# State update of a chunked delta-rule attention: one product chain for both halves of the heads, two copies of the state

## The chip, the core and the metric

The kernel runs on one core of a Trainium2 chip. The metric is the device time in microseconds (us), the median of three runs. The engines are PE (TensorE matmul; PEld is its weight load), DVE (VectorE), ACT (ScalarE), POOL (GpSimd) and SP (SyncE, whose queue issues the DMAs).

## The reference

Three stages follow one another. The first is a recurrent attention over 768 tokens for 4 batches of 8 heads, head size 48, with a state of 48 x 48 per head:

```python
k_n = k / (np.linalg.norm(k, axis=-1, keepdims=True) + 1e-06)
for t in range(S):
    kt, vt, bt = (k_n[:, :, t], v[:, :, t], beta[:, :, t, None])
    y[:, :, t] = np.einsum('bhd,bhde->bhe', q[:, :, t], state)
    v_old = np.einsum('bhde,bhd->bhe', state, kt)
    state = state + bt[:, :, :, None] * np.einsum('bhd,bhe->bhde', kt, vt - v_old)
```

Its output, as 3072 rows of 384, goes through a soft mixture of 8 experts (32 slots; the softmax over the tokens needs all of them first) and then through a feed-forward layer of width 2048 with a leaky ReLU. All arrays are float32.

## The kernel before

**Steps.** The 768 tokens are cut into 24 steps of 32. The partitions of most tiles are 4 batches times 32 tokens. The 8 heads are two halves of four, A = 0 and A = 1, and the batches two pairs, bp = 0 and bp = 1. Inside a step the recurrence over its 32 tokens is replaced by a triangular inverse, which does not depend on the state, so that one step is a chain of products. For each half:

- `ks_mm` (L406): ks(A), the step's keys times the state S[A], 16 matmuls, which the trace records as 32, added in PSUM (tile `ksu[A]`) to the values that `seed` (L399, ACT) put there.
- `z_of` (L423, L424 on ACT, L426 on DVE): the result is split into a high and a low fp16 part.
- `u_mm` (L432): the inverse, loaded into `tmb`, times z, 12 matmuls; then `u` is split in two fp16 parts too, u[:, 0] by L437 on ACT, and, up to step 19, u[:, 1] by a correcting matmul (L439) and a second ACT copy (L440). From step 20 on DVE makes u[:, 1] (L442).
- `s_mm` (L452): the state product. Keys (`khb`, high and low) times u (high and low) in three passes, `PASSB`: key high by u[:, 0], key low by u[:, 0], key high by u[:, 1]. Each pass has 4 heads times 2 batch pairs, so 8 matmuls on 64 rows each, alternately on rows 0 to 63 and 64 to 127 of the array (the two row tiles). They accumulate over all steps into two PSUM banks, `sps[0]` and `sps[1]`, one for each batch pair; both halves lie in each bank, in columns of their own.
- Two ACT copies (L456), 128x192 each, one for each bank, bring the half's new S to SBUF for the next step's `ks_mm` and `qs_mm`.
- `qs_mm` (L417, L413 from step 16) and `mu_mm` (L463, 24 matmuls for both halves) make the output `y`; `mu_mm` stands behind the last state product by `issue_after(last_s[0])`. L826 on ACT copies y; `logits` transposes it (L470), copies it (L473, ACT) and multiplies it by phi (L480), one step late. `soft` (among others L501, L510, L513, L517) does the running softmax of each four steps.

Beside the chain lies `gram` (L200, PE), eight steps ahead up to step 15, which yields the matrices to invert, and their copies (L207, L216).

**The inverse.** Four steps make a group. `solve(g)` inverts the matrices of a group on DVE (L241 to L312, with few ACT instructions, L250, L251, L316); it is a generator, and each `yield` ends a piece. solve(1) has 64 pieces: 8 up to the row of norms (L282), then one or two for each column j of the elimination (from column 3 on the first piece is L301 and L287, the second L305), at the end a transposition (L308) and the fp16 parts (L316 on ACT, L312 on DVE). `bs.run(n)` puts the next n pieces into the program. `DQ` tells how many at each of eight places of a step: place 0 is ahead of step 0, places 1 to 7 lie behind z(0), behind the DMAs, behind u(0), ahead of and between the two state products, behind the step's loads and at its end. At step 2 of a group `bs.run()` takes all that is left. So before the change solve(1) has 8 pieces ahead of step 0, 16 in step 0, 16 in step 1, and 24 in step 2; its result is first used in step 4. Solves of groups 2 to 5 begin in steps 3, 7, 11 and 15. From step 19 on DVE also decodes 64-bit weights (L560, L561, L563, L593 to L603).

**What sets the order.** The text of the program is not the order of an engine. A planner with a cost model of its own lists the instructions of each engine, by due time and priority: `tc.high_priority(offset=...)` moves a block ahead (dictionary `P`: `st`, the state product and its copies, 300; `mu` 300; `x` -30; `dma` -300), `tc.issue_after(i)` forbids an instruction to stand ahead of i on i's engine, and `behind(...)` does so for instructions noted in `end`. On the chip each engine keeps that order and waits where an operand isn't there.

**DMA.** All loads are issued by SP in one list: for each step two of keys and queries (`kqb`), four of the inverse (`tmb`, L380), four of the keys (`khb`, L369), one of keys and values (L329), and for later steps one to three more (L180, L189). `load_kq` is held until the last state product, `load_kv` until the last `u_mm` of half 0. From step 16 on the weights of the later stages are loaded (L571 and others; L632 brings the experts' w1 and w2, from step 20 on).

**After the attention** come the experts (L913, L932), fed by weights from memory, and the feed-forward layer (L1015, L1053 to L1068), which is a dense row of matmuls.

The loop over s in 0 to 23 contains, in this order: ks(0), preparation for step s + 2, `bs.run(dq[1])`, gram, ks(1), `step_dma`, `bs.run(dq[2])`, `qs_mm` of both halves, u(0), `bs.run(dq[3])`, u(1), both seeds, `soft`, `bs.run(dq[4])`, `s_mm` of half 0, `bs.run(dq[5])`, `s_mm` of half 1, loads, `bs.run(dq[6])`, the logits, `mu_mm`, L826, `bs.run(dq[7])`.

Of the kernel before, what the change touches and what calls it, by code (L numbers as in the profile page):

```python
# [8 lines left out]
F32 = mybir.dt.float32  # L9
# [3 lines left out]
AF = mybir.ActivationFunctionType  # L13
# [4 lines left out]
NST = 24  # L18
# [2 lines left out]
P = dict(st=300, mu=300, x=-30, dma=-300, split=-30, wi=-100)  # L21
DQ = (8, 5, 2, 2, 2, 2, 2, 1)
DQ_LAST = (8, 2, 3, 3, 3, 3, 3, 3)
DQ_NEXT = (0, 0, 1, 1, 1, 1, 1, 0)
DQ_FIRST = (0, 5, 2, 2, 3, 3, 3, 2)
SOFT_POOL = 5
# [18 lines left out]
PASSB = ((0, 0), (1, 0), (0, 1))  # L45


def drain(gen):
    for _ in gen:
        pass  # L50
# [3 lines left out]
def fused_kernel(ctx: ExitStack, tc: tile.TileContext, kq, kv, bu, phi, w1, w2, wi, wo, out):  # L54
    nc = tc.nc
    ve, sc, gp, pe, sy = nc.vector, nc.scalar, nc.gpsimd, nc.tensor, nc.sync

    def pool(stack, name, bufs, **kw):
        return stack.enter_context(tc.tile_pool(name=name, bufs=bufs, **kw))
# [14 lines left out]
    p_s = pool(at, "s", 2)  # L74
# [83 lines left out]
    def behind(*keys):  # L158
        st = ExitStack()
        for k in keys:  # L160
            if k in end:
                st.enter_context(tc.issue_after(end[k]))
        return st
# [170 lines left out]
    khs, last_s, tms = {}, [None], {}  # L334
# [20 lines left out]
    def step_k(s):  # L355
        khc = p_w.tile([128, 2, 384], F16, tag="khc", name="khc", bufs=KB)
        k1 = kvs[s // 2][:, s % 2, 0]
        sc.activation(k1, k1, AF.Copy, scale=64.0)
        kv1 = k1.rearrange("p (d a h) -> p a d h", a=2, h=4)
        k0, kl = [khc[:, l].rearrange("p (a d h) -> p a d h", a=2, h=4) for l in range(2)]  # L360
        end["k"] = sc.activation(k0, kv1, AF.Copy).ins
        after_solve(gp.tensor_tensor(kl, kv1, k0, SUB), s)
        khs[s] = khc.rearrange("p l (a x) -> p (l a) x", a=2)
# [19 lines left out]
    spf = [ps_st.tile([128, 512], F32, name=f"sps{i}") for i in range(2)]  # L383
    sps = [t[:, 0:384].rearrange("p (a h e) -> p a h e", a=2, h=4) for t in spf]
# [8 lines left out]
    S = {}  # L393
# [7 lines left out]
    def ks_mm(s, A):  # L401
        kb, st = kqb[s % 2], S[A]
        for hh in range(4):
            for b in range(4):
                bp, r = b // 2, slice(32 * (b % 2), 32 * (b % 2) + 32)
                end["ks"] = pe.matmul(ksu[A][32 * b:32 * b + 32, 48 * hh:48 * hh + 48], kb[:, bp, 0, r, 4 * A + hh], st[:, bp, hh, :],  # L406
                          start=False, stop=True, skip_group_check=True).ins
# [12 lines left out]
    def z_of(s, A):  # L420
        z = p_w.tile([128, 3, 192], F16, tag=f"z{A}", name="z")
        zp = ksu[A][:, 0:192]
        sc.activation(z[:, 0], zp, AF.Copy, scale=2.0 ** -6)  # L423
        end["z"] = sc.activation(z[:, 2], zp, AF.Copy, scale=2.0 ** -17).ins  # L424
        with behind("p") if s and s % 4 == 0 and s < 20 else nullcontext():
            end["zd"] = ve.scalar_tensor_tensor(z[:, 1], zp, 2.0 ** -6, z[:, 0], MULT, SUB).ins  # L426
        return z
# [14 lines left out]
            ve.scalar_tensor_tensor(u[:, 1], up, 32.0, u[:, 0], MULT, SUB)  # L442
        return u

    def s_mm(s, A, u):
        kb = khb[:, s % 2]
        for i, (a, b) in enumerate(PASSB):
            for hh in range(4):
                for bp in range(2):
                    q = slice(64 * bp, 64 * bp + 64)  # L450
                    with tc.issue_after(last_u[A].ins), tc.issue_after(last_s[0]) if last_s[0] is not None else nullcontext():
                        last_s[0] = pe.matmul(sps[bp][:, A, hh, :], kb[q, a, A, :, hh], u[q, b, hh, :],  # L452
                              start=False, stop=(s == NST - 2 and i == 2), skip_group_check=True).ins
        st = p_s.tile([128, 2, 4, 48], F32, tag=f"s{A}", name="st")
        for bp in range(2):
            sc.activation(st[:, bp], sps[bp][:, A], AF.Copy)  # L456
        S[A] = st

    def mu_mm(s, A, u, y):
        mv = tmb[s % 2][:, 2:4]  # L460
# [136 lines left out]
    def conv_wi(q):  # L597
        t = W[0, q] = place(3 * q, [128, 2, 768], F16)
        top = top_of(q < len(RAW), q)
        yield from from_f64(raw64.pop(("i", q)), top)  # L600
        sc.activation(t[:, 0], top, AF.Copy, scale=1024.0)
        yield
        ve.scalar_tensor_tensor(t[:, 1], top, 1024.0, t[:, 0], MULT, SUB)  # L603
        yield
# [36 lines left out]
    def load_late(s):  # L641
        with tc.issue_after(last_dma[0]):
            for x in LOADS.get(s, ()):
                if x == "w":
                    load_w()
                elif x == "i":
                    load_wi(n_wi[0])
                    n_wi[0] += 1
                else:
                    load_wo(n_wo[0])  # L650
                    n_wo[0] += 1

    def prep(s):
        step_m(s)
        step_ew(s)

    def pri(n):
        return tc.high_priority(offset=P[n]) if n in P else nullcontext()
# [78 lines left out]
    for s in range(NST):  # L737
        y = ps_y.tile([128, 8, 48], F32, tag="y", name="y")
        z, u = {}, {}
        dq = DQ_NEXT if s % 4 == 3 else DQ_FIRST if s and s % 4 == 0 else DQ if s < 15 else DQ_LAST  # L740

        def ks(A):
            if s:
                ks_mm(s, A)
            z[A] = z_of(s, A) if s else first_z[A]

        with behind("mu", "lp", "x"):
            ks(0)
        with behind("z"):
            if s + 2 < NST:  # L750
                prep(s + 2)
            if s + 2 < NST - 1:
                step_k(s + 2)
        with behind("zd"):
            bs.run(dq[1])
        if s + GA < NST:
            with behind("ks"):
                drain(gram(s + GA, masks))
        with behind("gm", "k"):
            ks(1)  # L760
        with behind("zd"):
            while masks:
                masks.pop()()
        if s in (3, 7, 11, 15):
            bs.add(solve(s // 4 + 2))
        if s == 19:
            load_late(s)
        if s + 1 < NST:
            with pri("dma"):
                step_dma(s + 1)  # L770
        if s != 19:
            load_late(s)
        for x, q in CONV.get(s, ()):
            bc.add(conv_wi(q) if x == "i" else conv_wo(q))

        def conv(n=1):
            if bc.q:
                with pri("wi"), tc.issue_after(solved[NG - 1]):
                    bc.run(n)
        with behind("zd"):  # L780
            bs.run(dq[2])
        if s:
            with behind("ks"):
                qs_mm(s, 0, y)
                qs_mm(s, 1, y)
        lg = logits(s - 1) if s else iter(())
        with behind("y"):
            u[0] = u_mm(s, 0, z[0])
            bs.run(dq[3])
            u[1] = u_mm(s, 1, z[1])  # L790
            with behind("u"):
                next(lg, None)
            if s < NST - 1:
                for A in range(2):
                    seed(s + 1, A)
            if s > 4:
                bf.run((0, 1, 2, 9)[s % 4])
            conv()
            bs.run(dq[4])
            if s < NST - 1:  # L800
                with pri("st"):
                    s_mm(s, 0, u[0])
            conv()
            bs.run(dq[5])
            if s < NST - 1:
                with pri("st"):
                    s_mm(s, 1, u[1])
        with tc.issue_after(tms[s + (s % 4 == 3 and s + 1 < NST)]):
            if s + 4 < NST:
                load_kv(s + 4, last_u[0].ins)  # L810
        with tc.issue_after(tms[s]):
            if s + 1 < NST - 1:
                with pri("dma"):
                    step_kdma(s + 1)
            if s + 10 < NST:
                load_kq(s + 10, last_s[0])
        conv()
        bs.run(dq[6])
        with behind("y"), tc.issue_after(last_s[0]):
            drain(lg)  # L820
            with pri("mu"), tc.issue_after(last_s[0]):
                for A in range(2):
                    mu_mm(s, A, u[A], y)
        with pri("x"):
            x = xg[s // 4 % 2][:, s % 4]
            end["x"] = sc.activation(x, y.rearrange("p h e -> p (h e)"), AF.Copy, scale=2.0 ** -12).ins  # L826
        if s % 4 == 2:
            bs.run()
        conv()
        bs.run(dq[7])  # L830
        if s and s % 4 == 0:
            bf.add(soft(s // 4 - 1))
            bf.run(1)
        free.extend(AVAIL.get(s, ()))
# [132 lines left out]
    with tc.high_priority(offset=CHAIN_PRIO), tc.issue_after(conv_ins[0]):  # L967
# [10 lines left out]
        for c in range(3):  # L978
            x = ss[:, c].unsqueeze(1).to_broadcast([128, 4, 32])
            h, l = [so16[:, i, c].rearrange("p (r x) -> p r x", r=4) for i in range(2)]  # L980
# [134 lines left out]
```

## Time and profile before

| what | us |
|---|---|
| median of three runs | 605.42 (601.75 to 609.35) |
| the profiled execution: its own time | 606.53 |
| its span, first to last instruction | 604.8 |
| outside the span | 1.7 |

PE is busy for 513.0 us of the span (85%), DVE 364.1 (60%), ACT 322.2 (53%), POOL 206.0 (34%). "PEclk" in a row is the granted TensorE clock as a share of 2.4 GHz: 1.00 is that level, 0.50 is 1.2 GHz, and what lies between is a stretch with both. Steps are told apart here by where ks(0) of a step begins; step 5, for example, goes from 105.61 to 117.32 us.

How such rows are read: a timeline row has the start, the time from the first to the last of the instructions that it merges, engine, line, what is written from what, and in brackets the idle time of the engine ahead of it and what ended it. A row of waits has the total of such idle times, how many there were and the longest. In rows by windows the busy times of the five engines stand behind the window's length.

### The profile page before, as it was taken

Reading aid. Unit: us, or ns where it says so; the run is one execution under the profiler, and the core shown is the slowest. Engines: PE = TensorE matmul, PEld = TensorE weight load, DVE = VectorE, ACT = ScalarE, POOL = GpSimd, SP = SyncE. Lnnn points to the kernel's source line nnn. Section 1 sums busy time; section 2 is a strip of 40 time slices with the busy share of each in tenths; the row PEclk is TensorE's granted clock in tenths of the full one; section 3 lists DMA queues with packets and bytes.
Section 4 is the critical chain, followed back from the end, with each engine's and each line's share of the span. In section 5 each row is a group of like instructions: output and inputs, shape, how many; then the busy total and the mean of one; then the engine's idle time right before and its main releaser. Section 6 shows DMA issues by size and latency. Waiting matters only on the chain.

```text
span 604.8 us, 18636 instructions
## 1 busy us (share of the span) xinstructions
PE 513.0 (85%) x7650; PEld 365.9 (60%) x7650; DVE 364.1 (60%) x1020; ACT 322.2 (53%) x783; POOL 206.0 (34%) x206
## 2 busy tenths in 40 slices
PE   7516787998987987888676978899999999999996
PEld 5515686877877875776674422566555555555553
DVE  3799778789887777899614453886423242333331
ACT  1325466566666655666542152566656555555552
POOL 9404122222313222224201000255555555454542
PEclk9665689899898787786687799999999999999999
DMA  9956658658766536786689999310101010010101
GB/s 221 227 124 152 144 137 194 155 140 191 171 172 161 131 90 156 201 260 128 193 267 420 395 404 418 143 53 1 53 0 54 2 42 12 1 54 1 53 1 52
DMA packets 70964, 87.27 MB, mean 144 GB/s; under 512 B 42720, under 2 KB 59360, under 8 KB 70880
## 3 DMA queue, kind: packets, MB, share of 16 engines
q1 hardware_dynamic: 70880, 86.09, 49.7%
q8 instruction: 60, 0.98, 0.7%
q14 instruction: 24, 0.20, 0.1%
HBM read 70.53 MB, written 4.72 MB: 124 GB/s over the span
## 4 chain that ended last, share of the span: by engine, by line
PE 63%; DVE 19%; ACT 8%; DMA 6%; issue 3%; SPq 0%; DVEq 0%; POOL 0%; ACTq 0%; POOLq 0%
PE ops L1015 31%; PE gm L200 4%; DMA arena<-in_w_dram 4%; PE hps L1053 3%; PE sps L452 3%; PE y L463 3%; PE xq L480 3%; PE ksu L406 3%; PE ksu L432 2%; DVE arena L301 2%; DVE arena L305 2%; DVE arena L287 2%; DMA kv<-in_kv_dram 2%; DVE arena L274 1%; ACT ksu L399 1%
## 5 line engine op out<-in xcount | busy, mean ns | idle before, releaser
L1068 POOL TENSOR_TENSOR gl<-gf,gh 128x512 f16<-128x512 f32 x96 | 113.7, 1200 | 151.4 <-ACT gh L1067 77.7
L1015 PE MATMUL ops<-late,gh 128*128 128x384 f16 x768 | 144.1, 326 | 0.0
L1062 DVE SCALAR_TENSOR_TENSOR gf<-hps,hs 128x512 f32<-128x512 f32 x96 | 62.5, 686 | 110.9 <-ACT hs L1061 110.7
L1015 PEld LDWEIGHTS <-gh 128*128 128x128 f16 x768 | 75.1, 98 | 53.6 <-ACT gh L1067 0.3
L1061 ACT ACTIVATE hs<-hps 128x512 f32<-128x512 f32 x96 | 53.0, 594 | 56.1 <-PE hps L1053 55.8
L1015 PE MATMUL ops<-late,gl 128*128 128x384 f16 x384 | 81.7, 326 | 0.0
L1067 ACT ACTIVATE gh<-gf 128x512 f16<-128x512 f32 x96 | 60.4, 629 | 26.7 <-DVE gf L1062 20.4
L352 POOL TENSOR_TENSOR vsz<-kv,nn 128x384 f32<-128x384 f32 x24 | 23.7, 988 | 101.9 <-issue 60.1
L200 PE MATMUL gm<-kqr,arena 128*64 128x64 f32 x640 | 44.2, 311 | 16.0 <-issue 16.0
L301 DVE TENSOR_TENSOR arena<-arena 128x81 f32<-128x81 f32 (+12 forms) x150 | 57.4, 383 | 0.1
L452 PE MATMUL sps<-u,khb 64*128 64x48 f16 x1104 | 35.1, 197 | 25.5 <-ACT st L456 20.6
L305 DVE TENSOR_TENSOR arena<-arena 128x81 f32<-128x81 f32 (+12 forms) x150 | 53.2, 355 | 0.0
L1015 PEld LDWEIGHTS <-gl 128*128 128x128 f16 x384 | 37.6, 98 | 24.8
L200 PEld LDWEIGHTS gm<-kqr,arena 128*64 128x64 f32 x640 | 41.2, 221 | 18.1 <-issue 16.2
L452 PEld LDWEIGHTS <-khb 64*128 64x128 f16 x1104 | 26.8, 115 | 38.2 <-issue 32.2
L406 PE MATMUL ksu<-st,kqb 128*32 128x48 f32 x1472 | 47.8, 258 | 2.5 <-issue 1.3
L346 POOL TENSOR_TENSOR tc<-mm,tc 128x256 f16<-128x256 f32 x24 | 19.4, 807 | 82.7 <-ACT tc L345 59.4
L287 DVE SCALAR_TENSOR_TENSOR arena<-arena 128x28 f32<-128x28 f32 (+27 forms) x186 | 47.0, 263 | 0.4
L406 PEld LDWEIGHTS ksu<-st,kqb 128*32 128x32 f32 x1472 | 39.6, 156 | 5.1 <-issue 1.4
L426 DVE SCALAR_TENSOR_TENSOR z<-ksu,z 128x192 f16<-128x192 f32 x48 | 16.8, 351 | 35.1 <-ACT z L424 35.0
L432 PE MATMUL ksu<-z,tmb 128*128 128x48 f16 x576 | 26.8, 195 | 9.2 <-DVE z L426 8.9
L432 PEld LDWEIGHTS <-tmb 128*128 128x128 f16 x576 | 23.8, 118 | 13.6 <-issue 10.8
(176 smaller groups left out, 856.9 us busy)
## 6 DMA issues: line engine op xcount, KB each, us to landing
we<-in_w_dram SPq DMA_DIRECT2D x22, 768.0 KB, 10.4
kv<-in_kv_dram SPq DMA_DIRECT2D x24, 384.0 KB, 4.5
kqb<-in_kq_dram SPq DMA_DIRECT2D x46, 192.0 KB, 4.3
kqr<-in_kq_dram SPq DMA_DIRECT2D x20, 384.0 KB, 4.8
arena<-in_w_dram SPq DMA_DIRECT2D x10, 768.0 KB, 8.3
tmb<-tc SPq DMA_DIRECT2D x96, 64.0 KB, 3.0
arena<-in_wi_dram SPq DMA_DIRECT2D x6, 768.0 KB, 6.4
raw<-in_wo_dram SPq DMA_DIRECT2D x6, 768.0 KB, 9.6
```

The source lines that it names most:

```text
L200: end["gm"] = pe.matmul(gm[64 * bp:64 * bp + 64, h, :], kb[:, k, bp, :, h], c[:, k, bp, :, :, h], start=(h == 0), stop=True, skip_group_ch ...
L287: end["p"] = ve.scalar_tensor_tensor(R[:, i, 0:j], R[:, j, 0:j], gu[:, i, j:j + 1], R[:, i, 0:j], MULT, ADD).ins
L301: ve.tensor_tensor(tv, gu[:, j + 2:, j:j + 1].to_broadcast([128, n, w]), R[:, j:j + 1, 0:w].to_broadcast([128, n, w]), MULT)
L305: ve.tensor_tensor(R[:, j + 2:, 0:w], R[:, j + 2:, 0:w], tv, ADD)
L406: end["ks"] = pe.matmul(ksu[A][32 * b:32 * b + 32, 48 * hh:48 * hh + 48], kb[:, bp, 0, r, 4 * A + hh], st[:, bp, hh, :], start=False, stop ...
L432: last_u[A] = pe.matmul(ksu[A][:, 192 + 48 * hh:240 + 48 * hh], tmb[s % 2][:, a, A, :, hh], z[:, b, 48 * hh:48 * hh + 48], start=False, st ...
L452: last_s[0] = pe.matmul(sps[bp][:, A, hh, :], kb[q, a, A, :, hh], u[q, b, hh, :], start=False, stop=(s == NST - 2 and i == 2), skip_group_ ...
L1015: pe.matmul(ops[t], g[:, 128 * t:128 * t + 128], w, start=(ft == 0 and i == 0), stop=(ft == 15 and i == 2))
L1061: sc.activation(hs, hps, AF.Copy, scale=2.0 ** -12)
L1062: gf_ins = ve.scalar_tensor_tensor(gf, hps, 0.01 * 2.0 ** -12, hs, MULT, MAX).ins
L1067: sc.activation(gh, gf, AF.Copy)
L1068: gp.tensor_tensor(gl, gf, gh, SUB)
```

## The change

Three things change. `s_mm` is called once in a step, behind the place where half 1's product stood, and writes the products of both halves in one chain, in the order half 0 passes 0 and 1, half 1 passes 0 and 1, half 0 pass 2, half 1 pass 2; the number of matmuls stays 48. S of both halves is one tile, copied by two ACT instructions of 128x384, one for each bank, instead of four of 128x192. And solve(1) gets other numbers of pieces: 10 in step 0 (4, 1, 1, 1, 1, 1, 1 at places 1 to 7) and 21 in step 1 (2, 4, 3, 3, 3, 3, 3), with 25 left for step 2; all other steps keep theirs.

```diff
+DQ_BEGIN = ((0, 4, 1, 1, 1, 1, 1, 1), (0, 2, 4, 3, 3, 3, 3, 3))
...
-    def s_mm(s, A, u):
+    def s_mm(s, u):
         kb = khb[:, s % 2]
-        for i, (a, b) in enumerate(PASSB):
+        for A, i in ((0, 0), (0, 1), (1, 0), (1, 1), (0, 2), (1, 2)):
+            a, b = PASSB[i]
             for hh in range(4):
                 for bp in range(2):
                     q = slice(64 * bp, 64 * bp + 64)
                     with tc.issue_after(last_u[A].ins), tc.issue_after(last_s[0]) if last_s[0] is not None else nullcontext():
-                        last_s[0] = pe.matmul(sps[bp][:, A, hh, :], kb[q, a, A, :, hh], u[q, b, hh, :],
+                        last_s[0] = pe.matmul(sps[bp][:, A, hh, :], kb[q, a, A, :, hh], u[A][q, b, hh, :],
                               start=False, stop=(s == NST - 2 and i == 2), skip_group_check=True).ins
-        st = p_s.tile([128, 2, 4, 48], F32, tag=f"s{A}", name="st")
+        st = p_s.tile([128, 2, 2, 4, 48], F32, tag="s", name="st")
         for bp in range(2):
-            sc.activation(st[:, bp], sps[bp][:, A], AF.Copy)
-        S[A] = st
+            sc.activation(st[:, bp].rearrange("p a h e -> p (a h e)"), spf[bp][:, 0:384], AF.Copy)
+        for A in range(2):
+            S[A] = st[:, :, A]
...
-        dq = DQ_NEXT if s % 4 == 3 else DQ_FIRST if s and s % 4 == 0 else DQ if s < 15 else DQ_LAST
+        dq = DQ_BEGIN[s] if s < 2 else DQ_NEXT if s % 4 == 3 else DQ_FIRST if s and s % 4 == 0 else DQ if s < 15 else DQ_LAST
...
             bs.run(dq[4])
-            if s < NST - 1:
-                with pri("st"):
-                    s_mm(s, 0, u[0])
             conv()
             bs.run(dq[5])
             if s < NST - 1:
                 with pri("st"):
-                    s_mm(s, 1, u[1])
+                    s_mm(s, u)
```

## Rows read from the trace of the kernel before

**Rows 1.** Waits of PE, 45 to 330 us: total us, times, longest us.
```profile
PE sps L452 <- ACT st L456: 20.6, 19, 1.3
...
PE ksu L432 <- DVE z L426: 8.9, 10, 3.1
PE mq L517 <- DVE acc L513: 4.5, 3, 1.6
```

**Rows 2.** Windows by stage: busy PE, PEld, DVE, ACT, POOL; PEclk, DMA share, GB/s.
```profile
48.84:320.79 271.95, 225.93 (x5688) 198.19 (x5688) 208.18 (x685) 162.71 (x491) 67.26 (x79) 0.82 0.68 174
320.79:381.00 60.21, 48.02 (x377) 20.67 (x375) 29.56 (x73) 21.70 (x45) 2.54 (x3) 0.90 0.99 399
```

**Rows 3.** Timeline of step 5: start, length, engine, line, what, count, [idle, releaser].
```profile
113.10 0.31 PE L452 MATMUL sps<-u,khb 64*128 64x48 f16 x8
...
113.43 0.48 ACT L473 ACTIVATE xt<-xq 128x384 f32<-128x384 f32 x1
...
113.80 0.50 ACT L399 ACTIVATE ksu<-vsz 128x384 f32<-128x384 f32 x1
...
114.21 0.56 ACT L456 ACTIVATE st<-sps 128x192 f32<-128x192 f32 x2
...
114.60 0.85 PE L452 MATMUL sps<-u,khb 64*128 64x48 f16 x24 [1.19 <-ACT st L456]
...
115.38 1.15 PE L463 MATMUL y<-u,tmb 128*128 128x48 f16 x24
...
117.32 0.39 PE L406 MATMUL ksu<-st,kqb 128*32 128x48 f32 x6
```

**Rows 4.** Waits of L452: steps 8 and 9; 16 to 18; 20 to 22.
```profile
  ACT st L456: 2.3, 2
...
  ACT st L456: 3.5, 3
...
  ACT st L456: 2.2, 3
```

**Rows 5.** Windows: steps 8 and 9; 16 to 18; 19 and 20.
```profile
138.17:161.55 23.38, 19.96 (x539) 17.86 (x537) 21.97 (x84) 15.04 (x48) 7.25 (x9) 0.88 0.85 200
...
233.93:266.32 32.39, 26.99 (x612) 23.90 (x610) 28.15 (x108) 18.79 (x60) 8.61 (x10) 0.76 0.75 198
266.32:296.29 29.97, 21.90 (x415) 17.13 (x415) 26.70 (x39) 18.50 (x49) 10.73 (x8) 0.67 0.71 196
```

**Rows 6.** Timeline of step 1, and where step 2 begins on DVE.
```profile
60.91 0.33 ACT L424 ACTIVATE z<-ksu 128x192 f16<-128x192 f32 x1
...
61.85 0.33 DVE L301 TENSOR_TENSOR arena<-arena 128x176 f32<-128x176 f32 x1
...
65.00 0.34 DVE L426 SCALAR_TENSOR_TENSOR z<-ksu,z 128x192 f16<-128x192 f32 x1
...
65.39 0.64 PE L432 MATMUL ksu<-z,tmb 128*128 128x48 f16 x12 [3.10 <-DVE z L426]
...
73.78 0.36 DVE L426 SCALAR_TENSOR_TENSOR z<-ksu,z 128x192 f16<-128x192 f32 x1 [3.94 <-ACT z L424]
```

**Rows 7.** Timeline of step 18: product, copies of S, next ks(0).
```profile
264.14 0.78 PE L452 MATMUL sps<-u,khb 64*128 64x48 f16 x24 [1.18 <-ACT st L456]
...
266.32 0.38 PE L406 MATMUL ksu<-st,kqb 128*32 128x48 f32 x2
...
267.79 1.15 ACT L316 ACTIVATE tc<-arena 128x256 f16<-128x256 f32 x2 [3.09 <-DVE arena L308]
...
268.84 0.53 ACT L456 ACTIVATE st<-sps 128x192 f32<-128x192 f32 x2
```

**Rows 8.** Windows from state product's end to next ks(0)'s end, steps 5, 6.
```profile
115.45:118.53 3.08, 3.08 (x64) 2.77 (x64) 1.40 (x4) 1.05 (x3) 0.71 (x1) 0.53 0.83 229
126.90:129.06 2.16, 2.16 (x64) 2.07 (x64) 2.06 (x9) 1.04 (x3) 0.79 (x1) 1.00 0.25 77
```

**Rows 9.** View of waits, the DMA queue of SP, steps 0 to 22.
```profile
SPq L369 <- PE sps L452: 34.1, 14, 6.0
```

## The prediction

> **What bounds the kernel now.** I read the windows by stage first, then the waits of PE, then the timeline of one step. The steps of the attention last 271.95 us, in which PE is busy 225.93 [rows 2]: PE is the busiest engine, and 46 us of its time there is idle. DVE follows with 208.18. Behind the steps 60.21 us run with the DMA engines 0.99 busy: that stretch starts when the steps end and is not touched. The waits say who makes PE idle: the largest by far is the state product behind its own copies, 20.6 us in 19 waits; then come u_mm behind the z of DVE, 8.9 us, and a transposition of the softmax behind DVE's L513, 4.5 us [rows 1].
>
> Step 5 shows the first wait [rows 3]. Half 0's product is written by 113.41 us (113.10 and 0.31 us). Half 1's product, into other columns of the same two banks, starts at 114.60 only, 1.19 us idle, released by the copy of half 0. That copy does not start until 114.21, because ACT works off the copy of L473 (113.43) and a seed (113.80) first. So on each step PE stands still for ACT, with half 1's operands at hand.
>
> **The wait removed.** In one chain no copy stands between the halves; with the same 48 matmuls it ends the wait earlier, at 114.60 + 0.85 - 1.19 = 114.26 [rows 3]. Of the 20.6 us, by place:
> - Steps 20 to 22: 2.2 us [rows 4]. Steps 19 and 20 together are held by DVE, 26.70 of 29.97 us busy with decoding [rows 5], and behind them the full DMA stretch follows. I count 0 (bounds 0 and 2.2).
> - Steps 16 to 18: 3.5 us [rows 4]. DVE is busy 28.15 of 32.39 us there [rows 5], with 4.2 us left over, not all of it where it is needed. I count half, 1.7 (0 to 3.5).
> - Steps 8 and 9: 2.3 us [rows 4], but DVE has only 23.38 - 21.97 = 1.4 us left [rows 5]. I count 1.4 (0 to 2.3).
> - The other 11 waits: 20.6 - 2.2 - 3.5 - 2.3 = 12.6 us. I count 12.3 (12.6 at most, and 6 if DVE took half of them too); step 0 has no logits that would cover the later copy, and keeps some 0.3 of its wait.
>
> Together 15.4 us.
>
> **The copies, later and wider.** Half 0's S now comes behind the whole chain, and ks(0) of the next step needs it. The cover is what PE does first: mu_mm, 115.38 to ks(0)'s start at 117.32, is 1.9 us with the logits in between [rows 3]. The copies: a pair of 128x192 takes 0.56 us, 0.33 for one by itself and 0.23 more, and L473, as wide as the new one and from PSUM too, takes 0.48 [rows 3]. Two of them thus take 0.48 + 0.23 x 2 = 0.94 us at most, if the pitch doubles with the width. ACT still has L473 and both seeds ahead of them: with 0.37 us from start to start (113.43 to 113.80) the second seed ends at 114.17 + 0.50 = 114.67, 0.4 us behind the chain's end; the copies end at 115.6, and ks(0) could start at 114.26 + 1.9 = 116.2. So they are hidden with 0.6 us to spare in step 5; in a step at full clock the cover is shorter by up to 0.9 us (below), and 0.3 us shows. I take -1.0 for all steps (0 to -9.5, half a microsecond in each of 19). ACT's busy time changes by less than 0.4 us a step, which costs nothing while it waits for PE in each step. The new tile has two buffers, so a copy overwrites the S that the step before read, long done: no wait there.
>
> **The pieces of the inverse.** In step 1 ACT's part of z(1) is done at 61.24 (60.91 and 0.33), but its DVE instruction runs at 65.00 only, behind all 16 pieces of step 0 and the 5 of place 1; PE waits 3.10 us for it at 65.39 [rows 6]. By the elimination's shapes z(1) stands behind piece 8 + 16 + 5 = 29; after the change it is behind 8 + 10 + 2 = 20, the one that ends where the row at 61.85 starts. So z(1) would run 65.00 - 61.85 = 3.15 us earlier, and u_mm, which could have started at 65.39 - 3.10 = 62.29, no longer waits: 3.1 us. The nine pieces go between z(1) of step 1 and z(0) of step 2, where DVE was idle 3.94 us [rows 6]; step 1's own product wait (20.6 / 19 = 1.1) shortens this to 2.8, and 3.15 us have to go in. I subtract 0.3: +2.8 (bounds 0, if all of it comes back in step 2, and 3.1). For the end of solve(1) one piece more in step 2 matters nothing; it is used two steps later.
>
> **What stood between the halves.** In three steps (11, 15, 19) the softmax's L517 was put between the two products and held PE 4.5 us behind L513 [rows 1]. With the product in one piece it has to stand elsewhere, ahead of mu_mm or behind it. I take a third, +1.5 (0 to 4.5).
>
> **The clock.** From the end of the product to the end of the next ks(0), the same instructions take 3.08 us at a granted 0.53 in step 5 and 2.16 at 1.00 in step 6 [rows 8], 0.9 us apart. Of the 16 such stretches of steps 2 to 14 and 16 to 18, 12 lie between 0.50 and 0.73 and four at 1.00. A denser product may raise some: I take +2.0 (0 to 11, 12 x 0.9).
>
> **What the new order upsets.** The planner lists all engines anew, and u_mm's other waits for z, 8.9 - 3.1 = 5.8 us in nine places [rows 1], can grow when PE comes sooner. I take -2.0 (+2 to -6, twice the present). The loads follow: the key loads of L369 stand on SP's queue behind the state product, 34.1 us in 14 waits [rows 9], with the next step's `tmb` loads behind them; as the product ends sooner, so do they. Nothing is added to any queue.
>
> **Sum.** 15.4 - 1.0 + 2.8 + 1.5 + 2.0 - 2.0 = 18.7 us. The profiled execution took 606.53 us (span 604.8 and 1.7 around it), 1.1 above the median; 587.8 on its scale, and 605.42 - 18.7 = 586.7 on the median's.
>
> **Rivals.**
> - The clock follows. If nearly all of the 12 stretches rise, 9 us more than I count come: 578. For it: the low stretches come right behind the wait. Against: so does step 6's, at 1.00 [rows 8]. The Trainium skill, "TensorE: Matmul & The Clock Gate", section on a second failure mode (psum-queue depth-cycling), says that short idles between groups of matmuls make the clock swing; by it, 578 would be the forecast, and the trace agrees in 12 stretches and not in four.
> - DVE becomes the bound. With 19 us less, DVE's 208.18 us stand in 253. At a group's end ACT stands at L316 until DVE has transposed: in step 18 for 3.09 us, with the copies of S behind it, begun at 268.84 where the product ended at 264.92 [rows 7]. Then only half 1's copy was late; now ks(0), which began at 266.32, would wait for 268.84 + 0.94, or 3.4 us. Three such ends give back 10 us: 597. For it: DVE has under 1.5 us left in steps 8 and 9. Against: over all steps it has 271.95 - 208.18 = 64 us left, 2.8 a step [rows 2].
> - One wait for another: ks(0) waits for the copies as long as half 1's product did, and of all of it only the 2.8 us of step 1 remain: 602.6. The Trainium skill, "TensorEngine Tiling (Array Packing)", section PSUM Bottleneck, warns of this: tiling makes the matmuls faster but not the way out of PSUM, and the copies may become the limit. Rows 3 speak against it, with the 0.6 us to spare.
> - Slower: the copies stand in ACT's list behind an instruction that itself waits, as in step 18, but in half of the steps. ks(0) is then 3.4 us late and 1.2 us are gained, 2.2 lost in each of 11 steps; the other eight gain 0.8. 605.4 + 24.2 - 6.4 - 2.8 = 620. It decides once the copies end more than 1.2 us later than the cover. Against: the copies keep their priority, and only step 18 shows this now.
>
> **How the numbers follow.** Forecast 0.50, the clock 0.13, DVE 0.22, one wait for another 0.09, slower 0.06. The forecast's own range is 580 to 594. For 8 in 10 I take in the clock and DVE: 575 to 600, with the last two cases and little else left out. About 2%, 12 us, is what a measurement of this kernel tells from no change. Faster than 593.3: all of the first two and a quarter of DVE's, 0.69; slower than 617.5: 0.06; between, 0.25.
>
> **What would show it.** Right: no wait of L452 behind L456; the chain of 48 in one run of about 1.7 us; steps at about 10 us instead of 11; z(1) of step 1 within 0.5 us of its ACT part, and no 3.1 us wait; the steps' stage near 253 us and the two stages behind it as long as now. Wrong: waits of L406 behind L456 of 10 us in total; waits of L432 behind z over 10 us; DVE at 0.9 of steps 4 to 14; or the DMA stretch longer by what the steps lose.

## The result, and the profile after

The changed kernel takes 572.0 us (median of 4 runs, 570.6 to 574.4) against 605.9 us before on the same chip (4 runs, 601.8 to 609.4): a ratio of 0.945, 95% interval 0.938 to 0.952. It is 33.9 us faster where 18.7 were forecast, and the time lies below the low end of the range, 575. The profiled execution took 570.64 us, with a span of 568.9; against the one before (606.53) that is 35.9 us. In three of the experiments below one execution lay more than 1.5% above the fastest of its kernel; medians and ratios are those of the others.

Line numbers move with the edit: L452 is now L454, the copies L456 are L458, L406 is L407, L426 and L432 are L427 and L433, L463 is L466, L480 is L483, L513 and L517 are L516 and L520.

First the waits of PE from 45 to 330 us, as in [rows 1].

```profile
PE ksu L433 <- DVE z L427: 4.3, 7, 1.2
...
PE sps L454 <- DVE u L443: 2.1, 2, 1.2
PE ksu L440 <- ACT u L438: 1.9, 4, 0.7
PE sps L454 <- issue: 1.6, 2, 1.4
PE sps L454 <- DMA khb<-khc: 1.6, 3, 0.7
...
PE mq L520 <- DVE acc L516: 0.5, 1, 0.5
```

No line has the copies L458 as its releaser any more: the 20.6 us in 19 waits are gone, and PE stands idle for S neither ahead of the product nor ahead of ks(0). L520's 4.5 us fell to 0.5, and u_mm's waits for z from 8.9 to 4.3.

Next the windows by stage, with the columns of [rows 2]; the third line is the stretch to the end of the span, and the fourth runs from ks(0) of step 1 to the start of ks(1) of step 23.

```profile
48.84:282.73 233.89, 211.94 (x5694) 189.82 (x5695) 204.75 (x685) 153.81 (x445) 66.04 (x76) 0.93 0.78 197
282.73:345.22 62.49, 49.04 (x369) 20.67 (x367) 27.64 (x72) 21.30 (x44) 2.83 (x6) 0.86 0.99 404
345.22:568.90 223.68, 216.39 (x1321) 128.79 (x1320) 91.29 (x140) 124.52 (x219) 113.79 (x96) 0.99 0.09 32
55.73:279.50 223.77, 202.57 (x5529) 182.09 (x5527) 198.16 (x665) 149.81 (x433) 61.90 (x71) 0.94 0.77 194
```

The same two cuts of the kernel before give, for its last stretch and for the steps:

```profile
381.00:604.80 223.80, 216.22 (x1321) 128.70 (x1318) 91.13 (x140) 124.47 (x218) 113.68 (x96) 1.00 0.09 32
56.84:318.76 261.92, 217.41 (x5529) 190.72 (x5527) 200.49 (x661) 158.35 (x476) 62.64 (x73) 0.83 0.68 171
```

The fourth line against the second of these is the comparison to read. The same 5,529 matmuls are in both. The stretch is 38.15 us shorter; PE's idle time in it falls from 44.51 (261.92 - 217.41) to 21.20 us, and its busy time from 217.41 to 202.57. So 23.3 us come from standing still less, and 14.8 from the same work done in less time. This is one execution of each kernel. PEclk goes from 0.83 to 0.94: if every moment is at one of the two levels, a mean of 0.83 over 261.92 us is 2 x 0.17 x 261.92 = 89 us at 1.2 GHz, and 0.94 over 223.77 is 27. Behind the steps the stretch under full DMA takes 62.49 us instead of 60.21, and the last one is unchanged.

Who lost what is in the groups of PE's instructions in these two stretches (busy us, mean ns of one | idle just before, and its releasers). Matmuls overlap, so the busy times of the groups add up to more than PE's. Before:

```profile
L406 PE MATMUL ksu<-st,kqb 128*32 128x48 f32 x1472 | 47.8, 258 | 2.5 <-issue 1.3 <-ACT st L456 1.2
L452 PE MATMUL sps<-u,khb 64*128 64x48 f16 x1056 | 33.4, 196 | 24.7 <-ACT st L456 19.8 <-DVE u L442 1.5 <-ACT u L437 1.4
L480 PE MATMUL xq<-xt,ph 128*32 128x128 f32 x132 | 29.2, 384 | 0.0
L432 PE MATMUL ksu<-z,tmb 128*128 128x48 f16 x528 | 24.5, 193 | 9.2 <-DVE z L426 8.9
...
L517 PE MATMUL mq<-ident,lt 128*128 128x128 f32 x4 | 1.6, 404 | 4.5 <-DVE acc L513 4.5
```

After:

```profile
L407 PE MATMUL ksu<-st,kqb 128*32 128x48 f32 x1472 | 40.7, 241 | 2.8 <-issue 1.1 <-DMA kqb<-in_kq_dram 0.9 <-ACT xg L826 0.8
L454 PE MATMUL sps<-u,khb 64*128 64x48 f16 x1056 | 28.7, 191 | 6.0 <-DVE u L443 2.1 <-issue 1.6 <-DMA khb<-khc 1.6
L433 PE MATMUL ksu<-z,tmb 128*128 128x48 f16 x528 | 24.6, 191 | 7.1 <-DVE z L427 4.3 <-issue 1.6 <-DMA tmb<-tc 0.9
...
L483 PE MATMUL xq<-xt,ph 128*32 128x128 f32 x132 | 21.8, 310 | 0.0
L520 PE MATMUL mq<-ident,lt 128*128 128x128 f32 x4 | 1.3, 323 | 0.0
```

The idle time ahead of the product falls by 18.7 us, ahead of L520 by 4.5, ahead of u_mm by 2.1. The logits (L483), of which not one instruction changed, take 21.8 us instead of 29.2: that is the clock. The product's own time falls by 4.7 us, while the mean of one hardly moves (196 to 191 ns): up to step 19 its matmuls now run in two stretches a step, of 16 and 32 with a correcting matmul (L440) between, where they ran in three, of 16, 8 and 24.

Last a step as it now runs, the timeline of step 2 (columns of [rows 3]).

```profile
74.32 0.46 PE L454 MATMUL sps<-u,khb 64*128 64x48 f16 x16
...
74.90 0.80 PE L454 MATMUL sps<-u,khb 64*128 64x48 f16 x32
...
75.23 0.49 ACT L476 ACTIVATE xt<-xq 128x384 f32<-128x384 f32 x1
...
75.60 0.91 ACT L400 ACTIVATE ksu<-vsz 128x384 f32<-128x384 f32 x2
...
75.64 0.98 PE L466 MATMUL y<-u,tmb 128*128 128x48 f16 x24
...
76.43 0.87 ACT L458 ACTIVATE st<-sps 128x384 f32<-128x384 f32 x2
76.55 0.62 PE L483 MATMUL xq<-xt,ph 128*32 128x128 f32 x4
...
76.97 0.26 PE L407 MATMUL ksu<-st,kqb 128*32 128x48 f32 x1
```

The chain of 48 lasts 1.38 us (74.32 to 75.70); 13 of the 23 take 1.37 to 1.41, the others up to 3.26, with the waits above in them. ACT works off the copy of the logits' input and both seeds, as in [rows 3], and copies S from 76.43 to 77.30, 0.87 us for both. PE has mu_mm and the logits meanwhile, and ks(0) of step 3 starts at 76.97 without a gap. The cover is just long enough: ks(0) starts 0.05 us behind the end of the first copy, while the second still runs. The same 0.05 us lie between the two in steps 4, 5, 11, 13 and 17: in these six ks(0) starts right behind the copy, but the logits are still running and PE is not idle.

### The profile page after: what moved, and what is told of

Read it like the earlier page. It is cut to its first block, busy times and chain, and to the rows that moved or that the text cites. A ratio compares the mean times of both kernels' runs of the same rounds, so it can differ in the third digit from the quotient of the medians.

```text
span 568.9 us, 18597 instructions
## 1 busy us (share of the span) xinstructions
PE 500.2 (88%) x7650; PEld 357.6 (63%) x7650; DVE 358.7 (63%) x1020; ACT 313.0 (55%) x737; POOL 205.2 (36%) x206
## 4 chain that ended last, share of the span: by engine, by line
PE 65%; DVE 14%; DMA 9%; SPq 4%; issue 3%; ACT 3%; DVEq 0%; ACTq 0%
PE ops L1015 33%; PE gm L201 5%; DMA we<-in_w_dram 4%; PE hps L1053 4%; PE ksu L407 3%; PE hn L913 3%; DMA khb<-khc 3%; DVE arena L302 3%; PE sps L454 2%; DVE arena L306 2%; SPq L381 2%; PE y L466 2%; DVE arena L288 2%; PE ksu L433 2%; PE son L932 2%
## 5 line engine op out<-in xcount | busy, mean ns | idle before, releaser
L302 DVE TENSOR_TENSOR arena<-arena 128x81 f32<-128x81 f32 (+12 forms) x150 | 55.8, 372 | 0.1
L306 DVE TENSOR_TENSOR arena<-arena 128x81 f32<-128x81 f32 (+12 forms) x150 | 51.3, 342 | 0.0
L353 POOL TENSOR_TENSOR vsz<-kv,nn 128x384 f32<-128x384 f32 x24 | 21.8, 910 | 81.7 <-ACT ksu L400 63.4
L288 DVE SCALAR_TENSOR_TENSOR arena<-arena 128x28 f32<-128x28 f32 (+27 forms) x186 | 49.5, 276 | 0.4
L407 PE MATMUL ksu<-st,kqb 128*32 128x48 f32 x1472 | 40.7, 241 | 2.8 <-issue 1.1
L407 PEld LDWEIGHTS ksu<-st,kqb 128*32 128x32 f32 x1472 | 34.8, 158 | 6.4 <-ACT xg L826 2.1
L454 PE MATMUL sps<-u,khb 64*128 64x48 f16 x1104 | 30.1, 192 | 6.0 <-DVE u L443 2.1
L208 ACT ACTIVATE arena<-gm 128x256 f32<-128x256 f32 x24 | 15.6, 651 | 34.7 <-PE gm L201 34.7
L454 PEld LDWEIGHTS <-khb 64*128 64x128 f16 x1104 | 24.7, 115 | 14.7 <-issue 7.6
L433 PE MATMUL ksu<-z,tmb 128*128 128x48 f16 x576 | 26.7, 192 | 7.1 <-DVE z L427 4.3
L1053 PE MATMUL hps<-cT,Gs 128*128 128x512 f16 x96 | 29.9, 379 | 2.1 <-DVE Gs L1008 2.1
```

Source lines behind the costliest of these rows:

```text
L288: end["p"] = ve.scalar_tensor_tensor(R[:, i, 0:j], R[:, j, 0:j], gu[:, i, j:j + 1], R[:, i, 0:j], MULT, ADD).ins
L302: ve.tensor_tensor(tv, gu[:, j + 2:, j:j + 1].to_broadcast([128, n, w]), R[:, j:j + 1, 0:w].to_broadcast([128, n, w]), MULT)
L306: ve.tensor_tensor(R[:, j + 2:, 0:w], R[:, j + 2:, 0:w], tv, ADD)
L1053: hp = pe.matmul(hps, Gs[:, 128 * ft:128 * ft + 128], cT[:, 512 * B:512 * B + 512], start=True, stop=True)
```

## The experiments

In the experiments "the stretch" is the one from ks(0) of step 1 to the start of ks(1) of step 23, and "time at the lower clock" is worked out from its PEclk as above.

**The pieces alone.** The kernel before with the new table of pieces for steps 0 and 1 and nothing else:

```diff
+DQ_BEGIN = ((0, 4, 1, 1, 1, 1, 1, 1), (0, 2, 4, 3, 3, 3, 3, 3))
-        dq = DQ_NEXT if s % 4 == 3 else ...
+        dq = DQ_BEGIN[s] if s < 2 else DQ_NEXT if s % 4 == 3 else ...
```

> Only the numbers of pieces in steps 0 and 1 change; the products and copies are as before. Theory (the wait between the halves, and the clock that falls behind it, carry the gain): the 20 us of waits of the state product behind its copies stay, the low clock stretches stay, and only the 3 us of step 1 go: ratio to before 0.993 to 0.998 (601 to 604 us). Rival (the pieces set off the rest: once step 1 is not late the clock and DVE run better in all later steps): 0.98 or less, under 594 us.

It took 599.9 us, ratio 0.990 (0.986 to 0.994): 6 us, over twice the 2.8 counted. Its stretch, and two of its waits:

```profile
56.30:311.90 255.60, 211.87 (x5529) 187.19 (x5527) 200.95 (x664) 158.23 (x476) 63.03 (x73) 0.86 0.68 178
...
PE sps L453 <- ACT st L457: 21.4, 19, 1.3
...
PE ksu L433 <- DVE z L427: 7.4, 12, 1.5
```

The product's wait is untouched, 21.4 us in 19 waits. The 3.1 us wait at which the edit aimed is gone, the longest one for z is now 1.5, and step 1 lasts 11.48 us instead of 14.95 (56.29 to 67.77; before, 56.84 to 71.79), 2.65 of the difference in idle time: as counted. Over the whole stretch PE is idle 43.73 us, only 0.8 less, since other steps have more (step 19 has 1.6 more), and busy 211.87, 5.5 less, at a PEclk of 0.86 instead of 0.83. That second part was not counted. Why so small a shift at the start raises the clock of later steps no run here settles.

**The chain alone.** The changed kernel with the old table of pieces (the two lines above taken out again).

> The one chain and the two copies, with the old numbers of pieces. Theory: all but the 3 us of step 1 is gained, ratio 0.947 to 0.955 (573 to 578 us), granted clock of the steps 0.90 or more. Rival (pieces): 0.96 to 0.98, 582 to 594 us.

It took 571.6 us, ratio 0.941 (0.935 to 0.947), the same as with the new table. Its stretch:

```profile
55.70:283.70 228.00, 205.80 (x5530) 184.05 (x5527) 196.58 (x665) 149.62 (x433) 59.89 (x71) 0.91 0.78 197
```

Step 1 lasts 13.8 us with the old table and 10.9 with the new one, so the pieces do shorten it. But most of this comes back at once: counted from the start of step 1, step 4 begins after 32.2 us with the old table and after 31.5 with the new one. With the new table DVE is busy 10.84 of the 10.87 us of step 1 and all 10.37 us of step 2, so the pieces that left step 1 fill step 2. The whole stretch takes 228.00 us against 223.77. But behind the stretch 569.8 - 283.7 = 286.1 us follow against 568.9 - 279.5 = 289.4: of the 4.2 us 3.3 are gone again by the end. Beside the chain the pieces are worth nothing that can be measured.

**The gap filled.** The kernel before, its wait left as it is, with 14 more matmuls of 128x128x128 in fp16 per step between the two halves' products. They go into 128 columns of y's bank that nothing uses, and nothing reads them.

```diff
+FILL = 14
...
-        y = ps_y.tile([128, 8, 48], F32, tag="y", name="y")
+        yf = ps_y.tile([128, 512], F32, tag="y", name="y")
+        y = yf[:, 0:384].rearrange("p (h e) -> p h e", h=8)
+        pe.matmul(yf[:, 384:512], id16, id16, start=True, stop=True, ...)
...
                     s_mm(s, 0, u[0])
+                    for _ in range(FILL):
+                        with tc.issue_after(last_s[0]):
+                            last_s[0] = pe.matmul(yf[:, 384:512], id16, id16, start=False, stop=True, ...).ins
```

> The kernel before, with 14 matmuls of 128x128 by 128 fp16 columns, whose result nobody reads, put on PE between the two state products, so that PE works through most of the 1.1 us while ACT copies as late as before. Theory (the clock falls because PE stands still there): the wait's time remains, about 0.3 us of it still as idle, the granted clock of the steps rises from 0.82 to 0.90 or more, and 10 to 14 us go: ratio 0.977 to 0.985 (591 to 596 us). Rival (the clock rises only because the steps are shorter or listed otherwise): clock 0.82 as before and 604 to 610 us, ratio 0.997 to 1.007, or slower by what the 14 matmuls last too long.

It took 585.8 us, ratio 0.968 (0.963 to 0.973): the added matmuls take some 26 us of PE, and the kernel is 20 us faster than before (605.9 on the same chip). Groups in its stretch, 241.00 us at a PEclk of 0.98 (10 us at the lower clock); L808 and L741 are the added matmuls:

```profile
L453 PE MATMUL sps<-u,khb 64*128 64x48 f16 x1056 | 33.5, 190 | 8.2 <-ACT st L457 5.5 <-DVE u L443 1.1 <-ACT u L438 0.4
...
L808 PE MATMUL y<-id 128*128 128x128 f16 x308 | 21.2, 220 | 0.9 <-issue 0.9
L481 PE MATMUL xq<-xt,ph 128*32 128x128 f32 x132 | 19.2, 283 | 0.0
L741 PE MATMUL y<-id 128*128 128x128 f16 x23 | 5.3, 230 | 0.0
```

The logits fall to 19.2 us. The product stays at 33.5, though the clock is high: its 4.7 us in the changed kernel are not the clock's. But u_mm's waits for z are nearly gone here as well (0.8 us): the planner's lists changed with the added work, so this run alone doesn't say how much is the clock. The next run does.

**The same matmuls elsewhere.** The same 14, issued behind mu_mm instead, so that the gap stays empty:

```diff
+FILL = 14
...
                     mu_mm(s, A, u[A], y)
+                for _ in range(FILL if s < NST - 1 else 0):
+                    with tc.issue_after(end["mu"]):
+                        end["mu"] = pe.matmul(yf[:, 384:512], id16, id16, start=False, stop=True, ...).ins
```

> The kernel before with the same 14 extra matmuls in each step, but put behind the output products, where PE does not stand still; the wait between the halves stays. Theory (what counts is PE's standing still between the halves): the 20 us of waits stay, the low clock stretches stay mostly (over 50 us of them in the steps, 89 before and 11 with the matmuls in the wait), and the extra matmuls cost most of their 20 us: 608 to 625 us, ratio 1.005 to 1.035. Rival (any additional matmuls lift the clock, or the list that the planner makes with them is what helped): low stretches under 30 us, 585 to 603 us, ratio 0.968 to 0.995.

It took 615.4 us, ratio 1.018 (1.014 to 1.022): some 10 us slower than the kernel before. Groups in its stretch, 270.90 us at a PEclk of 0.89 (60 us at the lower clock); L829 and L741 are the added ones:

```profile
L453 PE MATMUL sps<-u,khb 64*128 64x48 f16 x1056 | 33.2, 190 | 24.5 <-ACT st L457 23.1 <-ACT u L438 0.4
L829 PE MATMUL y<-id 128*128 128x128 f16 x309 | 30.5, 273 | 0.0
L481 PE MATMUL xq<-xt,ph 128*32 128x128 f32 x132 | 27.8, 371 | 0.0
...
L741 PE MATMUL y<-id 128*128 128x128 f16 x23 | 5.4, 235 | 0.0
```

The windows of both runs over this stretch, the filled one first:

```profile
57.10:298.10 241.00, 227.71 (x5860) 204.54 (x5858) 200.80 (x658) 158.38 (x476) 57.87 (x73) 0.98 0.72 185
```
```profile
58.10:329.00 270.90, 243.95 (x5859) 216.49 (x5858) 201.47 (x652) 158.94 (x476) 60.46 (x73) 0.89 0.65 168
```

The same work at two places is 29.9 us apart in this stretch. Here u_mm hardly waits for z in either run (0.8 us and none) and L518 not at all, so what differs is the gap: PE idle 26.95 us against 13.29 (13.7 apart) and busy 243.95 against 227.71 (16.2 apart). The same logits take 27.8 us against 19.2, the same added matmuls 30.5 against 21.2. With this added work an empty gap between the products thus costs its own length and about as much again in the clock of the other work. The gap is not all that sets the clock: it is there in the kernel before as in this run, with 89 and 60 us at the lower clock.

**The halves one after the other.** The changed kernel with the chain in the order of the kernel before: all of half 0, then all of half 1.

```diff
-        for A, i in ((0, 0), (0, 1), (1, 0), (1, 1), (0, 2), (1, 2)):
+        for A, i in ((0, 0), (0, 1), (0, 2), (1, 0), (1, 1), (1, 2)):
```

> The changed kernel, but the chain goes half by half: passes 0, 1, 2 of half 0, then 0, 1, 2 of half 1; still one chain with the two copies behind it. Theory (only the copy between the halves mattered): within 1% of the changed kernel, 570 to 577 us. Rival (putting half 1's first passes between covers the correction and copy that make u[:, 1] of half 0): pass 2 of half 0 waits 0.3 to 0.6 us in each step, 7 to 14 us more, 579 to 586 us, ratio 0.957 to 0.968.

571.8 us, ratio 0.942 (0.937 to 0.947): how the passes are interleaved plays no part that can be measured.

**The wait put back.** That kernel, with two ACT copies of half 0's columns between the halves. They write a scratch tile that nothing reads; the real copies stay behind the chain.

```diff
+            if (A, i) == (1, 0):
+                scr = p_s.tile([128, 2, 4, 48], F32, tag="scr", name="scr", bufs=1)
+                for bp in range(2):
+                    sc.activation(scr[:, bp], sps[bp][:, 0], AF.Copy)
```

> The changed kernel with the chain half by half and, between the halves, two ACT copies of half 0's sums (128x192 from each bank) into a tile that nobody reads. Pieces, the two wide copies and everything else stay as after the change; only the wait between the halves comes back. Theory (wait and clock carry the gain): 15 to 21 us of waits of the state product behind these copies, the granted clock of the steps back to 0.80 to 0.86, and 25 to 32 us lost: 596 to 604 us, ratio 0.984 to 0.997. Rival (much of the gain is the planner's other list, the wide copies or the pieces): only the wait's own 15 to 18 us are lost, 586 to 591 us, ratio 0.967 to 0.976.

600.6 us, ratio 0.994 (0.990 to 0.997), where it was 0.942 without them: some 30 us more. Its waits of PE:

```profile
PE sps L458 <- ACT scr L453: 21.9, 19, 1.3
...
PE ksu L433 <- DVE z L427: 8.1, 10, 2.0
PE mq L524 <- DVE acc L520: 5.2, 3, 2.3
```

and its stretch:

```profile
56.80:313.10 256.30, 214.96 (x5529) 189.30 (x5529) 200.02 (x660) 164.68 (x476) 61.92 (x73) 0.85 0.66 175
```

The wait brings everything back with it: the 19 waits, 77 us at the lower clock, and the softmax's transposition (L524) between the products with 5.2 us behind DVE. The two added copies are work for ACT as well (164.68 us busy, 149.81 in the changed kernel), but ks stands idle for 0.1 us in all, so it does not come late by them. The place between the products is not what makes the transposition wait: in both runs with added matmuls it stands there too and waits for nothing, and L511, whose result DVE has to read first, is listed earlier there. What is left of the gain, some 4 us, is near what the pieces bring alone.

**Four copies instead of two.** The changed kernel with S copied behind the chain in four 128x192 instructions:

```diff
-        for bp in range(2):
-            sc.activation(st[:, bp].rearrange("p a h e -> p (a h e)"), spf[bp][:, 0:384], AF.Copy)
+        for A in range(2):
+            for bp in range(2):
+                sc.activation(st[:, bp, A], sps[bp][:, A], AF.Copy)
```

> The changed kernel, but the copies behind the chain are four of 128x192 (half 0 first) instead of two of 128x384. Theory (one chain is what counts, the copies are hidden behind the output products either way): 570 to 576 us, within 1% of the changed kernel. Rival (fewer ACT instructions matter): 0.2 us more on ACT in each of 23 steps shows, 577 to 582 us.

572.9 us, ratio 0.945 (0.939 to 0.951), as with two. The number of copies has no effect that can be measured: they are covered.

**L517 moved by itself.** The kernel before with the softmax's part of the steps 3, 7, 11, ... placed in the program behind both products.

```diff
-            if s > 4:
-                bf.run((0, 1, 2, 9)[s % 4])
+            if s > 4 and s % 4 < 3:
+                bf.run((0, 1, 2)[s % 4])
...
                     s_mm(s, 1, u[1])
+            if s > 4 and s % 4 == 3:
+                bf.run(9)
```

> The kernel before, but in steps 7, 11, 15, 19 and 23 the softmax's part with L510, L513 and L517 comes behind both state products instead of ahead of them. Theory (L517 between the products held PE 4.5 us in three steps): those waits go, the waits of half 1 behind the copies come in these steps too (3 us), so 1 to 4 us less: ratio 0.993 to 0.999. Rival (a large part of the change's gain in steps 15, 16, 19 and 20, 16.6 us of 38, is this one reordering): 10 us or more, ratio 0.984 or less.

605.6 us, ratio 1.001 (0.999 to 1.003), and L517 still waits 4.5 us in three places between the products: the planner lists it there all the same. The edit did not do what it meant to, and says nothing of L517's price.

**Earlier loads.** Behind the steps PE waits for weights. Two further versions of the changed kernel load two pieces of them in steps 16 and 17; the second also moves the other loads of steps 16 to 18 behind those of the keys.

```diff
-LOADS = {16: "o", 17: "oi", 18: "ii", ...
+LOADS = {16: "ow", 17: "oiw", 18: "ii", ...
```

> The changed kernel with two loads of the experts' weights issued in steps 16 and 17 instead of later. Theory (what the steps gain beyond some 35 us is swallowed by the stretch that follows, since its DMA engines are 0.99 busy; two loads of 1.9 us moved ahead shorten it): 2 to 4 us less than after the change, 568 to 570 us, ratio 0.936 to 0.942. Rival (the stretch is bound by PE's own chain, or the early loads delay the keys and the inverse of steps 17 to 19): no gain or a loss, 571 to 576 us.

> The changed kernel with two weight loads in steps 16 and 17, and the loads of steps 16 to 18 issued behind the step's key loads instead of ahead of them. Theory (the earlier try lost by delaying the keys, 5.5 us of waits; behind the keys the loads are free and shorten the weights' stretch): 1 to 4 us less than the changed kernel, 568 to 571 us. Rival (the loads share the DMA engines with the next step's inverse and keys wherever they are issued): 572 to 576 us.

574.4 us (0.949, 0.946 to 0.952) and 575.7 us (0.950, 0.946 to 0.954): no gain. In the first the product waits 5.5 us for its keys (1.6 in the changed kernel), up to 3.9 at once: the early weights delay them. In the second u_mm's correcting matmul waits 5.2 us for ACT (1.9 in the changed kernel) and ks 3.0 us for its keys and queries.

**The changed kernel again**, beside the last two:

> The changed kernel once more, on the same chip as the two others, for comparison: 570 to 574 us, ratio 0.941 to 0.949 by either theory.

573.1 us, ratio 0.943 (0.936 to 0.949). No version that was tried is faster by more than the intervals leave open.

## Why the direction was right and the size was not

The wait was read rightly, and most of what the prediction said would show it did: no wait behind S's copies, a chain of 1.4 us where it said 1.7. The steps last 10.06 us (from 55.73 to 277.05 in 22 steps) where it said 10, but that number fits by luck: it said 10 instead of 11, and before they lasted 11.74 (56.84 to 315.07), from which 18.7 us in all would have left 10.9. The copies were sized rightly, 0.87 us for two where 0.94 was the most; of the 0.6 us to spare nothing was left in six steps, as shown above, but PE does not stand idle for them, so "one wait for another" (602.6) and the slower case (620) did not come. z(1) of step 1 stands behind the piece that was named: DVE ends it at 61.98 + 0.34, and u_mm's wait there is 0.90 us instead of 3.10 [rows 6]. It was to be within 0.5 us of its ACT part, however, and starts 1.70 us behind it (59.95 + 0.33).

Term by term, between the two profiled executions:

| term | counted | measured | from |
|---|---|---|---|
| wait of half 1's product | 15.4 | 18.7 | idle ahead of the product, 24.7 to 6.0 |
| the product's own time | none | 4.7 | 33.4 to 28.7 |
| L517 | 1.5 | 4.5 | idle 4.5 to 0.0 |
| pieces 2.8, planner -2.0 | 0.8 | 2.1 | idle ahead of u_mm, 9.2 to 7.1 |
| later copies | -1.0 | -0.3 | idle ahead of ks, 2.5 to 2.8, none of it behind the copies now |
| the clock | 2.0 | 10.1 | PE busy 14.8 less, without the product's 4.7 |
| other idle time of PE | none | -1.7 | the rest of the 23.3 |
| ahead of the stretch, and behind it | none | 1.1 - 3.4 | starts at 55.73, not 56.84; 289.4 us follow, not 286.0 |
| sum | 18.7 | 35.8 | 35.9 between the two times |

**The clock.** The step that failed most is "A denser product may raise some: I take +2.0 (0 to 11, 12 x 0.9)". It measured 10.1 us, near the upper bound; no row stood behind taking 2.0 of 11. The argument against it, that one of the stretches behind the wait ran at 1.00 all the same, counted four cases against twelve as if they spoke equally loud. The two runs with added matmuls, and the one with the wait put back, show that the gap itself lowers the clock: 60 and 77 us at the lower level with it, 10 and 27 without. With the gap gone PEclk is 1.00 over steps 4 to 14, from 0.90 before. The Trainium skill, "TensorE: Matmul & The Clock Gate", section on a second failure mode (psum-queue depth-cycling), says that short idles between groups of matmuls make the clock swing; the trace of these steps agrees. The rival beside which it stood, at 578, came nearest of all, and still had only the prediction's small terms beside it.

**DVE.** The second step that failed is the discount where DVE is nearly full: 0 for steps 20 to 22, as DVE held 19 and 20, half for 16 to 18, 1.4 for 8 and 9. Windows of the same steps after the change:

```profile
128.06:147.84 19.78, 17.91 (x534) 16.37 (x533) 18.10 (x74) 13.23 (x40) 5.93 (x8) 1.00 0.87 190
208.70:236.54 27.84, 24.75 (x608) 22.17 (x607) 26.98 (x108) 18.50 (x57) 9.02 (x12) 0.90 0.85 232
236.54:257.51 20.97, 18.00 (x415) 15.35 (x414) 17.68 (x35) 14.70 (x40) 9.41 (x9) 0.91 0.82 227
```

Against [rows 5] they are 3.6, 4.6 and 9.0 us shorter. In the second DVE is at 0.97, as close as was feared, but in the others its own work fell, from 21.97 to 18.10 us and from 26.70 to 17.68: the planner's list has other work of DVE there now. The decoding that left steps 19 and 20 went to the two steps behind them, where DVE had been nearly free: from ks(0) of step 21 to the end of the stretch it is busy 13.87 of 21.99 us, before 4.91 of 22.47. A window's DVE time is what the list put into it, not a floor under it. Over steps 4 to 14 DVE is now busy 100.88 of 111.15 us, which the prediction had named as a sign that it was wrong. The sign came and the harm did not: u_mm's waits for z fell.

**The smaller terms.** L517 was counted at a third of its 4.5 us because it "has to stand elsewhere"; it does, behind the logits in steps 11 and 15 and behind u_mm in step 19, and waits in none of these places. That the product would take less time in fewer stretches was not seen at all, though the step's timeline shows a stretch of 8 by itself [rows 3]. For the pieces, the 3.1 us of step 1 were right in kind (2.2 of them went), but with the chain in place 1.25 us of waiting for z came in step 2 instead: the lower bound, that it all comes back there, was the nearer one. That the stages behind the steps take as long as before was nearly right: 3.4 us are given back, 2.3 of them under full DMA.

**The range.** Its low end was set by the case of the clock alone, 578, less a little. The bounds in the text allowed 20.6 + 3.1 + 4.5 + 11 + 2 = 41.2 us, or 564. The wait, the clock and L517 all came out near the upper bound, and all three came back with the one wait; the low end let only the clock move.

## What to carry to other kernels

A gap of PE that comes back in each step can cost its length and then the clock of the other work: here 18.7 us of waiting and 10.1 of clock. To learn whether a gap does this, before any redesign, put matmuls that nobody reads into it, and the same ones somewhere else; the second run is needed, because the added work alone moved the clock too. Where two products share PSUM banks and the first one's copy holds up the second, issue both and copy behind them, provided that PE has work of its own to cover the copies.

When one wait is behind several rows (its own idle time, a low clock, something listed into the gap), add their upper bounds for the good end of the range.

## What the runs showed of the hardware

- Added work can make a kernel faster: 331 matmuls more, 26.5 us of PE time, took 20 us off. The logits, unchanged, took 29.2 us before, 19.2 with the gap filled, and 27.8 with the same matmuls elsewhere.
- Breaking up a row of short matmuls has a price, even at the high clock: the product's 1,056 matmuls take 33.5 us in three stretches a step (at a PEclk of 0.98) and 28.7 in two (at 0.94), with 190 and 191 ns for one.
- A copy from PSUM of twice the width took less than twice the time: two of 128x384 took 0.87 us in step 2, while two of 128x192 took 0.56 [rows 3].
